# Moving three pieces of work in the order of an attention and mixture-of-experts kernel

## The chip, the cores and the metric

The kernel runs on one core of one Trainium2 chip. The metric is the device time of one execution in microseconds (us). Five engines work side by side, each through its own instructions in order: TensorE (PE, matrix products and transposes), VectorE (DVE), ScalarE (ACT), GpSimd (POOL, which also issues the indirect transfers) and SyncE (SP, which issues plain transfers from its queue). They wait for each other by semaphores.

## The reference

Two stages follow each other. The first is a causal attention with decay, in blocks of 64 positions with a state carried between blocks, for 2 batches, 8 heads, 768 positions and 64 columns per head. Its result, laid out as 1536 tokens of 512 columns, is x of the second: each token goes to the one of 8 experts with the largest logit and comes back weighted by its probability. An expert takes tokens in their order up to its capacity (384).

```python
logits = x @ w_gate
expert_idx = np.argmax(logits, axis=1)
probs = np.exp(logits - logits.max(-1, keepdims=True))
probs /= probs.sum(-1, keepdims=True) + 1e-09
gate_w = probs[np.arange(N), expert_idx]
# tokens kept per expert, in order, up to the capacity: disp[e, pos[i]] = x[i]
h = np.maximum(np.einsum('ecd,edf->ecf', disp, w1), 0.0)
y = np.einsum('ecf,efd->ecd', h, w2)
out[i] = gate_w[i] * y[expert_idx[i], pos[i]]      # for every token that is kept
```

The weights are 8 experts with w1 of 512 by 1024 and w2 of 1024 by 512, in float32.

## The kernel before, in words

**Attention.** The 1536 tokens are worked in 12 ranks of 128 (`NTILE`), six to a batch. Round `s` of the loop in `attention()` works on several ranks at once: scores of rank `s+2` and masks of `s+1` ahead; `attend(s)` and `state(s)` for the rank itself; `turn(s-1)`, which multiplies the finished rank by a permuted identity and the gate's weights and so gives its rows and logits; `choose(s-1)` on VectorE (logits, maximum, index, one-hot `oh`); `rows(s-1)` and `soft(s-1)` on ScalarE (the rows are copied and the sum of exponentials taken); `place(s-2)` on TensorE and `placed(s-2)` on VectorE (the place of each token within its expert), and `scatter(s-2)`: ScalarE turns the places into integers (`slot`) and GpSimd issues an indirect transfer that writes 128 rows to the table `xs` in memory, sorted by expert. The last two ranks are chosen and scattered behind the loop, by the pieces `tail(0)`, `tail(1)` and `tail(2)`, which are put between the matmuls of expert 0's first tile; `count()` then counts the tokens of each expert, and `pad` writes zero rows behind them by indirect transfers.

**Weights.** Each expert has 8 pieces of 128 by 1024. `load_w(i)` loads piece `i` into one of four buffers; `split_hi(i)` rounds it on ScalarE to the precision in which TensorE multiplies at full speed; `split_lo(i)` subtracts on VectorE and keeps the remainder, and frees the buffer. Every product is taken as three: high by high, high by low, low by high. Expert 0's pieces are 0 to 7; 8 to 15 are expert 1's.

**Expert 0.** Its first two tiles of 128 tokens are worked alone, as `Solo` objects `first` and `second`: `turn` transposes the tile's rows, `rest` takes the low part of x, `up(0..3)` are the products with w1, `cross(0..1)` transposes the activations and splits them (`hh` on ScalarE, `hl` on VectorE), `down(0..3)` are the products with w2, `finish` scales by the gate and writes the tokens by an indirect transfer. `first` starts when the tokens of the early ranks have been scattered; `second` needs the rows of all ranks (`load_rows(0, 1)`).

**Experts 1 to 7.** Each takes 232 tokens at once. SyncE reads the expert's rows (`load_rows(e)`, behind the scatters and the pads of that expert), VectorE transposes them (`shuffle(e, g)`, two halves, the first with the token columns `tokens_of`), and `trans(e, g)` splits them into high (ScalarE) and low (VectorE). Expert 1's rows are turned while `second` is worked, those of the later ones during the expert before.

**Order.** The schedule is written out by hand: each engine runs its instructions in the order in which the program issues them. One engine never passes over an instruction that waits. On SyncE, the row reads and the loads of weights are one queue. The tiles of PSUM and of weights are in rings, so that a writer waits for the last reader of the buffer that it takes; `rank` and `st` share one tile, and `turn` writes one tile `tp` that `choose` and `rows` read.

Of the kernel before, what the change touches and what calls it, by code (L numbers as in the profile page):

```python
# [25 lines left out]
NTILE = NT // P  # L26
# [14 lines left out]
LO = {s: s - 5 for s in range(5, 12)}  # L41
# [3 lines left out]
def kernel(  # L45
# [50 lines left out]
    def load_w(i):  # L96
        if i >= E * NWP:
            return
        t = wraw_p.tile([P, WP], F32, tag="wraw", name="wraw")
        nc.sync.dma_start(out=t, in_=wp[i // NWP, i % NWP])  # L100
        raw[i] = t

    def split_hi(i):
        if i >= E * NWP:
            return
        hi = wsp_p.tile([P, WP], F32R, tag="whi", name="whi")
        nc.scalar.activation(out=hi, in_=raw[i], func=AF.Copy)  # L107
        wsp[i] = (hi, None)

    def split_lo(i):  # L110
        if i >= E * NWP:
            return
        t, hi = raw.pop(i), wsp[i][0]
        lo = wsp_p.tile([P, WP], F32R, tag="wlo", name="wlo")
        nc.vector.tensor_tensor(out=lo, in0=t, in1=hi.bitcast(F32), op=ALU.subtract)  # L115
        wsp[i] = (hi, lo)
# [136 lines left out]
    def attention():  # L253
        with ExitStack() as c2:
# [136 lines left out]
            first = Solo(0, spare, spare_ps)  # L391
# [16 lines left out]
            def decay_k(s):  # L408
                if s >= NTILE or s % NC == NC - 1:
                    return  # L410
                kd[s] = p2.tile([P, HP, 2, D], F32, tag="kd", name="kd")
                nc.gpsimd.tensor_tensor(
                    out=kd[s],
                    in0=ld[s, 1][:, 0:DM].rearrange("p (a r d) -> p a r d", a=HP, r=2),
                    in1=dt[:, :, :, P - 1:P].rearrange("p r a o -> p a r o").to_broadcast([P, HP, 2, D]),
                    op=ALU.mult,
                )
# [13 lines left out]
            def mask(s, rs=(0, 1)):  # L431
                if s >= NTILE:
                    return
                if 0 in rs:
                    pt[s] = p3.tile([P, 2, HP, P], F32, tag="pt", name="pt")
                for r in rs:
                    nc.vector.tensor_tensor(out=pt[s][:, r], in0=sc[s][r], in1=dt[:, r], op=ALU.mult)  # L437
# [29 lines left out]
            def carry(s):  # L467

                if s % NC in (0, NC - 1):
                    return  # L470
                tmp[s] = p2.tile([P, HP, D], F32, tag="tmp", name="tmp")
                for a in range(HP):
                    nc.scalar.activation(
                        out=tmp[s][:, a], in_=stt[s][:, a], func=AF.Copy, scale=qp[:, a, P - 1:P]
                    )

            def state(s):
                if s >= NTILE or s % NC == NC - 1:
                    return
                v = ld[s, 1][:, DM:2 * DM].rearrange("p (h d) -> p h d", h=H)  # L480
                for a in range(HP):
                    for r in range(2):
                        nc.tensor.matmul(  # L483
                            st[64 * r:64 * r + 64, a], lhsT=kd[s][:, a, r], rhs=v[:, 2 * a + r],
                            start=True, stop=True,
                        )
                stt[s + 1] = p2.tile([P, HP, D], F32, tag="stt", name="stt")
                if s % NC == 0:
                    nc.vector.tensor_copy(stt[s + 1], st)
                else:  # L490
                    nc.vector.tensor_tensor(out=stt[s + 1], in0=tmp[s], in1=st, op=ALU.add)
# [25 lines left out]
            def choose(s):  # L517
                if s < 0:
                    return
                lg[s] = sm.tile([P, E], F32, tag="l", name="l")  # L520
                nc.vector.tensor_reduce(
                    out=lg[s], in_=tp[s][:, :, P:P + E].rearrange("p k e -> p e k"),
                    axis=mybir.AxisListType.X, op=ALU.add,
                )
                m8[s] = sm.tile([P, 8], F32, tag="m8", name="m8")
                nc.vector.max(out=m8[s], in_=lg[s])
                nc.vector.max_index(out=i8_all[:, s], in_max=m8[s], in_values=lg[s])
                oneh[s] = sm.tile([P, E], F16, tag="oh", name="oh")
                nc.vector.tensor_tensor(  # L529
                    out=oneh[s], in0=nr[s], in1=i8_all[:, s, 0:1].to_broadcast([P, E]), op=ALU.is_equal  # L530
                )
# [17 lines left out]
            def place(s):  # L549
                if s < 0:  # L550
                    return
                nc.tensor.matmul(rank, lhsT=upper, rhs=oneh[s], start=True, stop=False)
                nc.tensor.matmul(rank, lhsT=ones, rhs=cum[s], start=False, stop=(s < EARLY))
                if s >= EARLY:
                    nc.tensor.matmul(rank, lhsT=ones, rhs=more, start=False, stop=True)

            def placed(s):
                if s < 0:
                    return
                pr = sm.tile([P, E], F32, tag="pr", name="pr")  # L560
                nc.vector.scalar_tensor_tensor(
                    out=pr, in0=rank, scalar=1.0, in1=oneh[s], op0=ALU.mult, op1=ALU.mult,
                    accum_out=sraw[:, s:s + 1],
                )
# [11 lines left out]
            def scatter(s):  # L576
                if s < 0:
                    return
                nc.scalar.activation(out=slot[:, s:s + 1], in_=sraw[:, s:s + 1], func=AF.Copy)  # L579
                i = nc.gpsimd.indirect_dma_start(  # L580
                    out=xs, out_offset=bass.IndirectOffsetOnAxis(ap=slot[:, s:s + 1], axis=0),
                    in_=xg_all[:, s], in_offset=None, bounds_check=E * STR - 1, oob_is_err=False,
                )
                apart(i, "xs", s >= EARLY)
# [14 lines left out]
            load(5, 0)  # L599
            tokens()  # L600
            for s in range(NTILE):
                place(s - 2)
                carry(s)
                mask(s + 1, (0,))
                placed(s - 2)
                mask(s + 1, (1,))
                scatter(s - 2)
                decay_k(s + 1)
                if s == NTILE - 1:
                    first.rest()  # L610
                if s in LO:
                    split_lo(LO[s])
                if s > 0:
                    attend(s)
                    state(s)
                if s in HI:
                    split_hi(HI[s])
                turn(s - 1)
                choose(s - 1)
                if s == EARLY + 1:  # L620
                    shift()
                rows(s - 1)
                soft(s - 1)
                if s == NTILE - 2:
                    first.turn()
                score(s + 2)
                if s > 0:
                    load(s + 4, 1)
                for i in LOAD.get(s, ()):
                    load_w(i)  # L630
                decay_q(s + 2)
                add_up(s - 1)
                load(s + 6, 0)
                if s == EARLY - 1:
                    number(slice(NTILE - 2, NTILE))
                if s == EARLY + 1:
                    load_rows(0, 0)
            s = NTILE - 1
# [37 lines left out]
            pad(1, 0)  # L676
            pad(1, 1)
            load_rows(1)
            split_lo(7)
            first.cross(0)  # L680
            split_hi(8)
            first.up(3)
            split_lo(8)
            load_w(11)
            first.down(0)
            first.cross(1)
            split_hi(9)
            split_lo(9)
            load_w(12)
            first.down(1)  # L690
        return first

    def ffn(first):
        with ExitStack() as c2:
# [10 lines left out]
            def shuffle(e, g):  # L705
                if e >= E:
                    return
                if g == 0:
                    tokens_of(e)
                    xf[e] = xf_p.tile([P, KD, RS], F32, tag="xf", name="xf")  # L710
                    xhl[e] = xt_p.tile([P, KD, 2, SLOT], F32R, tag="xhl", name="xhl")
                ks = slice(2 * g, 2 * g + 2)
                nc.vector.transpose(  # L713
                    out=xf[e][:, ks].rearrange("p k (t c) -> p k t c", c=32),
                    in_=rw[e].rearrange("p t (k c) -> p k t c", k=KD)[:, ks],
                )
# [47 lines left out]
            split_w(11)  # L764
            load_w(15)
            second.up(3)
            second.down(0)
            second.cross(1)
            shuffle(1, 0)
            trans(1, 0)  # L770
            shuffle(1, 1)
            trans(1, 1)
# [283 lines left out]
```

## Time and profile before

Three runs took 251.21, 251.28 and 251.78 us; the median is 251.28.

| | |
|---|---|
| profiled execution | 252.51 us |
| its span (first to last instruction) | 250.8 us |
| granted TensorE clock, mean | 0.996 |
| TensorE busy | 237.1 us (95%) |
| VectorE busy | 172.4 us (69%) |
| ScalarE busy | 144.5 us (58%) |
| GpSimd busy | 87.1 us (35%) |
| memory read, written | 50.37 MB, 11.22 MB |

The span is cut by what the core does: ranks of attention to about 59 us, expert 0's first tile with the last choices to about 76, its second tile to about 90, then seven experts of some 21 to 22 us each. Busy times are per engine and overlap. An engine's idle time stands in brackets in a timeline, with the instruction whose end released it. In the chain of waits each piece released the next one.

### The profile page before, as it was taken

The page shows a single profiled execution, that of the slowest core. Times are in us where ns is not written, and L with a number is a line of the kernel's source. Part 1 is how long each engine was busy: PE and PEld are TensorE (multiplying, and loading weights), DVE is VectorE, ACT ScalarE, POOL GpSimd, SP SyncE. Part 2 cuts the span into 40 slices and gives each one's busy share as a digit, 9 for nine tenths or more (in the row PEclk, how much of TensorE's full clock was granted, in tenths as well). Part 3 has the DMA queues.
Part 4 walks back from the last instruction along what each step waited for, and adds up shares of the span by engine and source line. Part 5 has one row for each costly group of instructions (what it writes and reads, how often), then busy time and mean ns, then how long its engine had stood idle before and what let it go on. Part 6 is the DMA issues. An engine that isn't in the chain of part 4 may idle for free.

```text
span 250.8 us, 4968 instructions
## 1 busy us (share of the span) xinstructions
PE 237.1 (95%) x1838; PEld 199.6 (80%) x1838; DVE 172.4 (69%) x323; ACT 144.5 (58%) x267; POOL 87.1 (35%) x105
## 2 busy tenths in 40 slices
PE   7899999999899989999999999999999999999990
PEld 3688888787888979879877977987897788789880
DVE  4555589996474476797679679768866876896400
ACT  2216666788453456568557656855765585586220
POOL 8585769995273502005101600510250030011031
PEclk9999999999999999999999999999999999999998
DMA  5999999958526938867578769859775889462010
GB/s 113 409 370 406 398 381 411 413 176 282 182 71 133 355 122 260 201 220 238 175 236 305 262 141 324 252 178 284 242 249 153 323 236 305 148 231 78 1 54 15
DMA packets 27006, 58.52 MB, mean 233 GB/s; under 512 B 6392, under 2 KB 13562, under 8 KB 26976
## 3 DMA queue, kind: packets, MB, share of 16 engines
q1 hardware_dynamic: 22896, 50.89, 62.5%
q0 software_dynamic: 3376, 7.24, 7.6%
q8 instruction: 16, 0.26, 0.4%
q10 hardware_dynamic: 704, 0.02, 0.2%
q14 instruction: 14, 0.11, 0.1%
HBM read 50.37 MB, written 11.22 MB: 246 GB/s over the span
## 4 chain that ended last, share of the span: by engine, by line
PE 45%; issue 15%; DVE 13%; DMA 11%; ACT 9%; POOL 2%; SPq 1%; POOLq 1%; DVEq 0%; ACTq 0%
PE y L828 13%; PE h L796 10%; DVE wlo L115 6%; DMA wraw<-in_wp 5%; PE h L800 5%; ACT whi L107 5%; PE tp L504 4%; PE sc L429 4%; PE x L449 3%; DMA qk<-in_qkv 3%; DVE hf L806 2%; PE x L457 2%; PE st L483 2%; DVE xhl L724 2%; PE solo_ps L219 1%
## 5 line engine op out<-in xcount | busy, mean ns | idle before, releaser
L115 DVE TENSOR_TENSOR wlo<-wraw,whi 128x1024 fp32r<-128x1024 f32 x64 | 80.9, 1273 | 12.0 <-ACT whi L107 10.1
L796 PE MATMUL h<-xhl,whi 128*128 128x464 f32 x224 | 73.3, 380 | 2.1 <-DVE xhl L724 2.1
L107 ACT ACTIVATE whi<-wraw 128x1024 fp32r<-128x1024 f32 x64 | 66.2, 1047 | 8.7 <-DMA wraw<-in_wp 8.6
L800 PE MATMUL h<-xhl,wlo 128*128 128x232 f32 x224 | 60.2, 269 | 0.0
L183 POOL DMA_INDIRECT out<-y,ti x13 | 15.6, 1196 | 118.3 <-ACT y L837 116.4
L796 PEld LDWEIGHTS h<-xhl,whi 128*128 128x128 f32 x224 | 42.0, 188 | 8.7 <-DVE xhl L724 2.9
L800 PEld LDWEIGHTS h<-xhl,wlo 128*128 128x128 f32 x224 | 42.7, 190 | 0.3
L828 PE MATMUL y<-whi,hh 128*128 128x512 f32 (+1 forms) x104 | 41.1, 396 | 0.0
L828 PE MATMUL y<-whi,hl 128*128 128x512 f32 (+1 forms) x104 | 41.1, 395 | 0.0
L828 PE MATMUL y<-wlo,hh 128*128 128x512 f32 (+1 forms) x104 | 40.9, 393 | 0.0
L809 ACT ACTIVATE hh<-hf 128x464 fp32r<-128x464 f32 x28 | 16.6, 592 | 33.8 <-DVE hf L806 33.8
L810 DVE SCALAR_TENSOR_TENSOR hl<-hf,hh 128x464 fp32r<-128x464 f32 x28 | 18.0, 642 | 18.4 <-ACT hh L809 18.4
L828 PEld LDWEIGHTS y<-whi,hl 128*128 128x128 f32 (+1 forms) x104 | 18.6, 179 | 5.7
L828 PEld LDWEIGHTS y<-wlo,hh 128*128 128x128 f32 (+1 forms) x104 | 18.6, 179 | 5.3
L828 PEld LDWEIGHTS y<-whi,hh 128*128 128x128 f32 (+1 forms) x104 | 18.6, 178 | 5.3
L806 DVE TENSOR_TENSOR hf<-h,hf 128x464 f32<-128x464 f32 x28 | 17.8, 636 | 4.0 <-ACT hf L805 3.3
L580 POOL DMA_INDIRECT xs<-xg,slot x12 | 14.2, 1180 | 11.1 <-ACT slot L579 7.3
L437 DVE TENSOR_TENSOR pt<-sc,dt 128x512 f32<-128x512 f32 x24 | 16.2, 687 | 2.5 <-PE sc L429 2.0
L134 POOL DMA_INDIRECT xs<-zero,padi x14 | 16.1, 1146 | 4.3 <-issue 4.0
L805 ACT ACTIVATE hf<-h 128x464 f32<-128x464 f32 x28 | 15.2, 543 | 2.3 <-PE h L800 2.2
L723 ACT ACTIVATE xhl<-xf 128x464 fp32r<-128x464 f32 x14 | 8.3, 591 | 11.9 <-DVE xf L713 11.9
L513 ACT ACTIVATE xg<-tp 128x512 f32<-128x512 f32 x12 | 7.2, 598 | 13.5 <-DVE oh L529 11.7
(133 smaller groups left out, 349.6 us busy)
## 6 DMA issues: line engine op xcount, KB each, us to landing
wraw<-in_wp SPq DMA_DIRECT2D x64, 512.0 KB
qk<-in_qkv SPq DMA_DIRECT2D x12, 512.0 KB
kv<-in_qkv SPq DMA_DIRECT2D x12, 512.0 KB
rw<-xs SPq DMA_DIRECT2D x28, 128.0 KB
xs<-xg SPq DMA_DIRECT2D x1, 514.0 KB
rw<-xs SPq DMA_DIRECT2D x2, 257.0 KB
xs<-zero,padi POOLq DMA_INDIRECT x14, 3.5
out<-y,ti POOLq DMA_INDIRECT x13, 4.0
```

What stands on the lines that cost most here:

```text
L107: nc.scalar.activation(out=hi, in_=raw[i], func=AF.Copy)
L115: nc.vector.tensor_tensor(out=lo, in0=t, in1=hi.bitcast(F32), op=ALU.subtract)
L134: i = nc.gpsimd.indirect_dma_start(out=xs, out_offset=bass.IndirectOffsetOnAxis(ap=padi[:, e, t:t + 1], axis=0), in_=zero, in_offset=None, ...
L183: i = nc.gpsimd.indirect_dma_start(out=out, out_offset=bass.IndirectOffsetOnAxis(ap=ti[e][0:m, t:t + 1], axis=0), in_=y[0:m], in_offset=No ...
L437: nc.vector.tensor_tensor(out=pt[s][:, r], in0=sc[s][r], in1=dt[:, r], op=ALU.mult)
L796: nc.tensor.matmul(ps[:, f, 0:2 * SLOT], lhsT=wh[:, k, fs], rhs=x2[:, k], start=(k == 0), stop=False, skip_group_check=True,)
L800: nc.tensor.matmul(ps[:, f, 0:SLOT], lhsT=wl[:, k, fs], rhs=x2[:, k, 0], start=False, stop=(k == KD - 1), skip_group_check=True,)
L805: nc.scalar.activation(out=hf, in_=ps[:, :, SLOT:2 * SLOT], func=AF.Copy)
L806: nc.vector.tensor_tensor(out=hf, in0=ps[:, :, 0:SLOT], in1=hf, op=ALU.add)
L809: nc.scalar.activation(out=hh, in_=hf, func=AF.Relu)
L810: nc.vector.scalar_tensor_tensor(out=hl, in0=hf, scalar=0.0, in1=hh.bitcast(F32), op0=ALU.max, op1=ALU.subtract)
L828: nc.tensor.matmul(yp[t][0:m], lhsT=a[:, f, tsl], rhs=b[:, f], start=(p == 0 and f == 0 and n == 0), stop=(p == 3 and f == 1 and n == 2),)
```

## The change

Three things are moved; no instruction is added or taken away.

1. In the last round of the loop (`s` = 11), `place(9)`, `placed(9)` and `scatter(9)` come behind `attend(11)` instead of ahead of it (`carry`, `mask` and `decay_k` do nothing in that round), and `split_lo(6)` comes behind `choose(10)` instead of ahead of the attention. `first.rest()` is then the round's first work on VectorE.
2. Behind the loop, `split_lo(7)` is issued behind `first.up(3)` instead of ahead of `first.cross(0)`, and `split_lo(8)` behind `first.cross(1)` instead of ahead of `first.down(0)`. `load_w(12)` comes two steps earlier in the program, behind `split_lo(8)`; `split_lo(9)` comes behind `first.down(1)`.
3. In expert 0's second tile, `shuffle(1, 0)`, the first half of expert 1's transposition, comes ahead of `second.down(0)` and `second.cross(1)`.

```diff
@@ -599,24 +599,31 @@
             load(5, 0)
             tokens()
             for s in range(NTILE):
-                place(s - 2)
-                carry(s)
-                mask(s + 1, (0,))
-                placed(s - 2)
-                mask(s + 1, (1,))
-                scatter(s - 2)
-                decay_k(s + 1)
-                if s == NTILE - 1:
+                if s < NTILE - 1:
+                    place(s - 2)
+                    carry(s)
+                    mask(s + 1, (0,))
+                    placed(s - 2)
+                    mask(s + 1, (1,))
+                    scatter(s - 2)
+                    decay_k(s + 1)
+                    if s in LO:
+                        split_lo(LO[s])
+                else:
                     first.rest()
-                if s in LO:
-                    split_lo(LO[s])
                 if s > 0:
                     attend(s)
                     state(s)
+                if s == NTILE - 1:
+                    place(s - 2)
+                    placed(s - 2)
+                    scatter(s - 2)
                 if s in HI:
                     split_hi(HI[s])
                 turn(s - 1)
                 choose(s - 1)
+                if s == NTILE - 1:
+                    split_lo(LO[s])
                 if s == EARLY + 1:
                     shift()
                 rows(s - 1)
@@ -676,18 +683,18 @@
             pad(1, 0)
             pad(1, 1)
             load_rows(1)
-            split_lo(7)
             first.cross(0)
             split_hi(8)
             first.up(3)
-            split_lo(8)
+            split_lo(7)
             load_w(11)
             first.down(0)
             first.cross(1)
+            split_lo(8)
+            load_w(12)
             split_hi(9)
+            first.down(1)
             split_lo(9)
-            load_w(12)
-            first.down(1)
         return first
 
     def ffn(first):
@@ -764,9 +771,9 @@
             split_w(11)
             load_w(15)
             second.up(3)
+            shuffle(1, 0)
             second.down(0)
             second.cross(1)
-            shuffle(1, 0)
             trans(1, 0)
             shuffle(1, 1)
             trans(1, 1)
```

## Rows read from the trace of the kernel before

**Rows 1.** TensorE's waits from 56 us to the end: us in total, times, longest.
```profile
PE h L796 <- DVE xhl L724: 2.1, 3, 0.9
```
**Rows 2.** Timeline of TensorE: start, us, instructions, idle time before.
```profile
59.35 0.17 PE L552 MATMUL st<-oh,upper 128*128 128x8 f16 x1 [0.59 <-DVE m L526]
61.12 0.18 PE L502 MATMUL tp<-num,warm 128*128 128x8 f16 x1
64.05 0.17 PE L552 MATMUL st<-oh,upper 128*128 128x8 f16 x1 [0.78 <-DVE oh L529]
64.74 0.17 PE L502 MATMUL tp<-num,warm 128*128 128x8 f16 x1
76.17 0.63 PE L200 MATMUL solo_ps<-ident,rw 128*128 128x128 f32 x4 [0.61 <-DMA rw<-xs]
91.93 0.47 PE L796 MATMUL h<-xhl,whi 128*128 128x464 f32 x1 [0.94 <-DVE xhl L724]
```
**Rows 3.** Timeline of VectorE, last round of the loop.
```profile
61.09 0.69 DVE L205 TENSOR_TENSOR solo_xl<-solo_ps,solo_xh 128x512 fp32r<-128x512 f32 x1 [1.29 <-ACT slot L579]
62.02 1.21 DVE L115 TENSOR_TENSOR wlo<-wraw,whi 128x1024 fp32r<-128x1024 f32 x1
63.14 0.18 DVE L521 TENSOR_REDUCE l<-tp 128x8 f32<-128x32 f32 x1
63.84 0.17 DVE L529 TENSOR_TENSOR oh<-tp,i 128x8 f16<-128x8 f32 x1
64.31 0.17 DVE L561 SCALAR_TENSOR_TENSOR pr<-st,oh 128x8 f32<-128x8 f32 x1 [0.31 <-PE st L555]
```
**Rows 4.** Timeline of ScalarE, last round of the loop.
```profile
60.41 0.57 ACT L202 ACTIVATE solo_xh<-solo_ps 128x512 fp32r<-128x512 f32 x1
64.09 0.60 ACT L513 ACTIVATE xg<-tp 128x512 f32<-128x512 f32 x1 [1.29 <-DVE oh L529]
```
**Rows 5.** Timeline of GpSimd: indirect transfers issued.
```profile
68.98 1.97 POOL L580 DMA_INDIRECT xs<-xg,slot  x1 [1.69 <-ACT slot L579]
71.26 1.97 POOL L134 DMA_INDIRECT xs<-zero,padi  x1 [0.30 <-DVE solo_hl L232]
73.53 0.97 POOL L134 DMA_INDIRECT xs<-zero,padi  x1 [0.30 <-issue]
...
140.32 0.99 POOL L134 DMA_INDIRECT xs<-zero,padi  x1 [0.30 <-issue]
```
**Rows 6.** Timeline of VectorE beside those transfers.
```profile
68.86 1.22 DVE L115 TENSOR_TENSOR wlo<-wraw,whi 128x1024 fp32r<-128x1024 f32 x1
70.21 0.69 DVE L232 TENSOR_TENSOR solo_hl<-solo_ps,solo_hh 128x512 fp32r<-128x512 f32 x1
71.16 1.23 DVE L115 TENSOR_TENSOR wlo<-wraw,whi 128x1024 fp32r<-128x1024 f32 x1 [0.26 <-ACT whi L107]
...
140.74 1.23 DVE L115 TENSOR_TENSOR wlo<-wraw,whi 128x1024 fp32r<-128x1024 f32 x1 [0.30 <-ACT whi L107]
```
**Rows 7.** Timeline of SyncE's queue: the row reads.
```profile
73.27 0.33 SPq L167 DMA_DIRECT2D rw<-xs  x1
76.82 1.81 SPq L152 DMA_DIRECT2D rw<-xs  x4
```
**Rows 8.** Chain of waits: start, us, what.
```profile
79.22 4.51 DMA wraw<-in_wp
```
**Rows 9.** Timeline of ScalarE, second expert's weights.
```profile
83.87 1.06 ACT L107 ACTIVATE whi<-wraw 128x1024 fp32r<-128x1024 f32 x1 [0.27 <-DMA wraw<-in_wp]
```
**Rows 10.** Timeline of VectorE from the second tile to expert 1.
```profile
77.52 0.69 DVE L205 TENSOR_TENSOR solo_x<-solo_ps,solo_x 128x512 fp32r<-128x512 f32 x1 [1.88 <-ACT solo_x L202]
84.97 1.23 DVE L115 TENSOR_TENSOR wlo<-wraw,whi 128x1024 fp32r<-128x1024 f32 x1 [0.64 <-ACT whi L107]
86.89 0.69 DVE L232 TENSOR_TENSOR solo_hl<-solo_ps,solo_hh 128x512 fp32r<-128x512 f32 x1 [0.70 <-ACT solo_hh L231]
87.94 0.71 DVE L713 STREAM_TRANSPOSE xf<-rw 128x512 f32<-128x512 f32 x1
```

## The prediction

> **What bounds the kernel now.** I began with the page: TensorE is busy 95% of the span at full clock, so what is left to win there is its gaps. TensorE's waits come next. Behind the eleventh round of the loop the largest entry, 2.1 us in three waits, is the experts' matmul held by VectorE's `xhl` [rows 1]; the timeline puts 0.94 us of it at 91.93, the start of expert 1. Three other gaps stand in the same timeline: 0.59 at 59.35 and 0.78 at 64.05 (ranks waiting for a choice) and 0.61 at 76.17 (the second tile of expert 0 waiting for its row read) [rows 2]. Then the chain of waits, followed back from 91.93: VectorE's transposition and low part for expert 1, weight piece 11 and its load at 79.22 [rows 8], SyncE's row read of expert 1 at 76.82 [rows 7], two `pad` transfers on GpSimd [rows 5], and before them the last two choices. So the stretch from 59 to 92 us is bound by one chain across all engines, which touches TensorE at four gaps, 2.92 us in sum. All three edits lie on it.
>
> **Step 1, the loop's last round.** Before, `place(9)` waits on TensorE till 59.35, then attention and `turn(10)` follow, the latter at 61.12 [rows 2]. After, `attend(11)` starts when the transposes are over, at 59.35 - 0.59 = 58.76, and nothing that it reads is late; with the same 1.77 us for attention and rank, `turn(10)` starts near 60.5. That alone gives nothing: `choose(10)` is on VectorE, in order, behind `first.rest()` and `split_lo(6)`. There the first low part of x starts at 61.09, since it waits for ScalarE's copy (60.41 + 0.57) [rows 3, 4]; this is unchanged. At 62.02 `split_lo(6)` begins, and the choice starts at 63.14 [rows 3]. After, the place of `split_lo` is taken by `placed(9)`, which came earlier before: one 0.17 us instruction [rows 3] and its readout, together 0.2 as I take them. `choose(10)` then starts at 62.2 and, at the same 0.87 us (63.14 to 63.84 + 0.17), ends at 63.07 instead of 64.01: 0.94 us sooner. `split_lo(6)` runs from 63.1 to 64.3, beside matmuls, and delays `placed(10)` to 64.3, which is where it stands now (64.31) [rows 3].
>
> Not all of the 0.94 reaches TensorE. `turn(11)` (64.74) writes the tile that `rows(10)` reads, so it waits for that copy to end, 64.09 + 0.60 [rows 2, 4]. ScalarE is in order: `slot(9)` now waits for `placed(9)` till 62.3, `split_hi(7)` stands behind it (the same copy takes 1.06 in rows 9), so `rows(10)` starts near 63.4, not at 63.1. `turn(11)` comes at 64.0: gain **0.72 us**. Everything behind it (third part of `up`, last choice, `count`) follows TensorE and shifts alike. Bounds: 0.94 if ScalarE doesn't hold it, zero if `slot(9)` is some 0.7 later than I think. The moved `scatter(9)` issues near 62.8 instead of its old place ahead of the choices; its successors on GpSimd, `add_up(10)` and `scatter(10)`, are wanted by `place(11)` past 66 only. SyncE's load of weight 10, which needs `split_lo(6)`, slips about 1.1 us; its row reads are not due until 71, so they lose nothing.
>
> **Step 2, the low parts 7 and 8.** An indirect transfer on GpSimd takes 0.97 to 0.99 when nothing is in the way. The last scatter at 68.98 and the first pad at 71.26 take 1.97 [rows 5]. Each began just behind the start of a `split_lo` on VectorE (68.86, 1.22; 71.16, 1.23), and each ends 0.84 to 0.87 us behind that `split_lo`'s end [rows 5, 6]. The pad at 73.53 had no `split_lo` running and took 0.97. One that has begun isn't caught: at 140.32 a pad took 0.99 though a `split_lo` began at 140.74 [rows 5, 6]. So the rule of the rows: a transfer that begins inside a `split_lo` waits for its end, then needs 0.84. By it, after the edit:
> - Last scatter: 68.98 - 0.72 = 68.26, no `split_lo` beside it, ends 69.24. First pad 0.30 later, 69.54 to 70.5. `split_lo(7)` is still issued by VectorE as soon as the crossing's low part `hl` is done (70.21 + 0.69 - 0.72 = 70.18), since nothing it reads is late: it does not stay behind the third `up`. It catches the second pad, which begins at 70.8, holds it till 71.4, and the pad ends at 72.2 instead of 74.50.
> - Row read of expert 0's second tile: 73.27 less 0.72 less 0.99 = 71.56 [rows 7]. Its data were what TensorE got at 76.17; 1.71 earlier is 74.46. TensorE itself arrives at 76.17 - 0.61 - 0.72 = 74.84. The gap of **0.61 us** goes whole, with 0.38 to spare; what is late next there is TensorE's own work.
> - Row read of expert 1: 76.82 less 2.3 = 74.5, and weight 11 behind it loads from 76.9 instead of 79.22; at the same 4.51 us [rows 8] it lands at 81.4.
> - `split_lo(8)` follows the second crossing. VectorE stood idle for 1.88 us ahead of the second tile's low part of x at 77.52 [rows 10]; less the 0.61 that TensorE no longer waits, 1.27 are left for the 1.23 of `split_lo(8)`. It just fits; were it late by x, the tile's first `up` would lose at most x, and I take nothing.
>
> The Trainium skill speaks against step 2. Its page "SBUF — State Buffer", section "Who interferes with whom", says that a two-input `tensor_tensor` did not stall DMAs in its probe, because it takes only the read side of the port pair shared with GpSimd and the writing of descriptors needs the write side (marked as inferred); the same section says that such an instruction does contend with a GpSimd instruction that reads SBUF. By the first sentence moving `split_lo` frees no transfer and the sum would lose the 0.61; by the second, and by the two 1.97 us transfers of this trace, it does. I go by the rows.
>
> **Step 3, the shuffle ahead of the crossing.** Now VectorE does `split_lo(11)` (84.97, 1.23), the crossing's low part (86.89, 0.69), the token columns and the first transposition (87.94, 0.71), and from 87.94 a chain of two transpositions, copies and low parts releases TensorE at 91.93 [rows 2, 10]. After, weight 11 is there in time: its high part, which waited 0.27 for the load [rows 9], starts at 83.60 - 1.33 = 82.3, the low part ends near 84.6 (it began 1.10 behind the high part), the token columns take at most 0.44 (86.89 to 87.94 less the 0.61 after which the next can follow a low part) [rows 10], and the transposition is done at about 85.7. The crossing's low part is due at 86.89 - 1.33 = 85.56: at most 0.15 late, and I take nothing for it. The transposed rows are there 2.9 us earlier (88.65 to 85.7), so the chain, with nothing else on its way, would end near 89.0. TensorE wants it at 91.93 - 0.94 - 1.33 = 89.66: the **0.94 us** go as well. By bounds: none if the chain came 1.6 us later than I reckon, 0.94 at most.
>
> **Sum.** 0.72 + 0.61 + 0.94 = 2.27 us. The profiled execution took 252.51 (span 250.8 and 1.7 around it), so 250.24 in its terms; the runs have a median of 251.28, and I take the same amount off: **249.0 us**. Behind 92 us the instructions are the same, TensorE runs on without a gap but for the other 1.2 us of those three waits [rows 1], and loads are asked for by freed buffers, so the shift should carry to the end.
>
> **Rivals.**
> - *The rows' rule is a coincidence; transfers aren't freed (the skill's first sentence).* The row read moves by 0.72 only, the 0.61 gap stays, weight 11 moves by 0.72, and the shuffle pushes the crossing's low part back by up to 0.43. Gain 0.72 + 0.94 less 0.43 at worst: 1.2 to 1.7, time 249.6 to 250.1. For it: nothing in the trace; against it: both 1.97 transfers.
> - *The front gives nothing.* If ScalarE's order (`slot(9)`, `split_hi(7)`, `rows(10)`) costs all of step 1, the other two remain: 1.55, 249.7.
> - *More than that.* The other two waits of [rows 1], 1.2 us later on, depend on when loads land; if the shift happens to remove them, 248.0.
> - *The gain is given back at an expert's boundary*: an earlier chain asks for loads that land when they landed before. 250.6 to 251.6. Against it: the row reads and loads of this stretch are queued behind transfers that move too.
> - *Slower.* Five more expert boundaries each read new rows and weights behind pads. If the new phase of pads against `split_lo` made each of them wait as at 91.93, five times 0.94 less the 1.2 now there, 3.5 us, would come on: 252.5. It decides from 0.46 us more per boundary (2.27 over five). Against it: these stretches keep their own order on every engine.
>
> **How the numbers follow.** Chances: forecast 0.62 (own range 248.6 to 249.5), more 0.08, rule a coincidence 0.08, front gives nothing 0.09, given back 0.08, slower 0.05. A difference counts from 0.3%, 0.75 us, which is about what can be told from no change: the first four are faster (0.87), then same 0.08, slower 0.05. The range from 248.2 to 250.2 leaves out most of the last two cases and about half of "more".
>
> **What would show it.** In the changed profile: `attend(11)` ahead of the rank with no 0.59 gap; `choose(10)` starting near 62.2 and `turn(11)` near 64.0; last scatter and first pad under 1.05 us, second pad near 1.4; no gap ahead of the second tile's transposes; weight 11's load near 76.9; no gap in expert 1's first piece; then the same work some 2.3 us earlier. It would be wrong if the scatters still take 1.97 with no `split_lo` beside them, if `turn(11)` stays at 64.7, or if a wait for `xhl` longer than 0.9 appears at a later boundary.

## The result, and the profile after

The changed kernel takes 248.72 us (median of 4 runs, 247.08 to 249.20) against 251.25 for the kernel before; the ratio is 0.9884, with an interval from 0.9839 to 0.9928. On another chip it was 248.13 against 251.15, 0.9896 (0.9849 to 0.9943). 249.0 had been forecast. The profiled execution took 248.73 (span 246.9) against 252.51 (250.8): 3.8 less, of which only 2.85 belong to the three steps, as the table below shows.

TensorE's waits from 56 us to the end (us in total, times, longest): of the six behind [rows 1, 2], one is left.

```profile
PE st L552 <- DVE oh L529: 0.5, 1, 0.5
```

The timeline of TensorE, for [rows 2]: attention follows the transposes with no gap, the rank comes behind it, the second tile's transposes and expert 1's third pair of matmuls (89.25) wait for nothing.

```profile
58.77 1.09 PE L449 MATMUL x<-pt,kv 128*64 128x128 f32 x16
60.39 0.18 PE L552 MATMUL st<-oh,upper 128*128 128x8 f16 x1
63.09 0.17 PE L552 MATMUL st<-oh,upper 128*128 128x8 f16 x1 [0.47 <-DVE oh L529]
63.98 0.17 PE L502 MATMUL tp<-num,warm 128*128 128x8 f16 x1
74.64 0.60 PE L200 MATMUL solo_ps<-ident,rw 128*128 128x128 f32 x4
89.25 0.38 PE L803 MATMUL h<-xhl,whi 128*128 128x464 f32 x1
```

VectorE's timeline in the loop's last round and beside the last choices, for [rows 3, 6]. The choice starts at 62.17 instead of 63.14, right behind `placed(9)`; `split_lo(6)` runs behind it, `split_lo(7)` right behind the crossing's low part.

```profile
62.10 0.15 DVE L561 SCALAR_TENSOR_TENSOR pr<-st,oh 128x8 f32<-128x8 f32 x1
62.17 0.19 DVE L521 TENSOR_REDUCE l<-tp 128x8 f32<-128x32 f32 x1
62.95 1.22 DVE L115 TENSOR_TENSOR wlo<-wraw,whi 128x1024 fp32r<-128x1024 f32 x1
...
69.44 0.69 DVE L232 TENSOR_TENSOR solo_hl<-solo_ps,solo_hh 128x512 fp32r<-128x512 f32 x1 [1.26 <-ACT solo_hh L231]
70.05 1.22 DVE L115 TENSOR_TENSOR wlo<-wraw,whi 128x1024 fp32r<-128x1024 f32 x1
```

ScalarE's timeline, for [rows 4]: `slot(9)` waits for `placed(9)`, `split_hi(7)` stands behind it, and `rows(10)` comes at 63.35, not at 64.09.

```profile
62.29 0.21 ACT L579 ACTIVATE slot<-sraw 128x1 int32<-128x1 f32 x1 [0.73 <-DVE pr L561]
62.40 1.04 ACT L107 ACTIVATE whi<-wraw 128x1024 fp32r<-128x1024 f32 x1
63.35 0.58 ACT L513 ACTIVATE xg<-tp 128x512 f32<-128x512 f32 x1
```

GpSimd's timeline, for [rows 5]: the last scatter and first pad take 0.99 and 0.97 instead of 1.97; the second pad, which begins inside `split_lo(7)`, ends at 72.11, 0.84 behind that instruction's end (71.27).

```profile
68.21 0.99 POOL L580 DMA_INDIRECT xs<-xg,slot  x1 [1.69 <-ACT slot L579]
69.51 0.97 POOL L134 DMA_INDIRECT xs<-zero,padi  x1 [0.30 <-issue]
70.79 1.32 POOL L134 DMA_INDIRECT xs<-zero,padi  x1 [0.30 <-issue]
```

SyncE's queue, for [rows 7, 8]: the second tile's row read is issued at 71.01 (73.27 before), expert 1's at 74.47 (76.82), weight 11's load at 76.89 (79.22).

```profile
71.01 0.33 SPq L167 DMA_DIRECT2D rw<-xs  x1
74.47 1.82 SPq L152 DMA_DIRECT2D rw<-xs  x4
76.33 0.45 SPq L157 DMA_DIRECT2D wt<-xs  x1
76.89 14.66 SPq L100 DMA_DIRECT2D wraw<-in_wp  x7
```

VectorE ahead of expert 1, for [rows 10]: the transposition ends at 85.29, just as the crossing's low part falls due (85.31), and the chain ends at 88.52, before TensorE asks.

```profile
83.00 1.23 DVE L115 TENSOR_TENSOR wlo<-wraw,whi 128x1024 fp32r<-128x1024 f32 x1 [0.25 <-issue]
...
84.58 0.71 DVE L720 STREAM_TRANSPOSE xf<-rw 128x512 f32<-128x512 f32 x1
85.31 0.69 DVE L232 TENSOR_TENSOR solo_hl<-solo_ps,solo_hh 128x512 fp32r<-128x512 f32 x1
...
87.88 0.64 DVE L731 TENSOR_TENSOR xhl<-xf,xhl 128x464 fp32r<-128x464 f32 x1 [0.66 <-ACT xhl L730]
```

For the comparison of executions I read from each TensorE timeline when the work of a stage starts. The attention's start-up shifts from one execution to the next (by up to 1.6 us in those here), so each column is set against the start of `state(10)`'s matmuls, which is put at the 56.49 us of before. A boundary, below, is the change from one expert to the next. The last two columns belong to the later boundaries: the time from expert 2's start to expert 7's, and TensorE's idle times (its brackets) at the starts.

| execution | `turn(11)` | second tile | expert 1 | expert 2 | expert 2's start to 7's | waits at the starts of experts 2 to 7 |
|---|---|---|---|---|---|---|
| before | 64.74 | 76.17 | 90.19 | 112.85 | 109.32 | 0.39, 0.74 |
| before, again (e4) | 64.74 | 75.58 | 90.32 | 112.98 | 109.32 | 0.22, 0.86 |
| changed | 63.90 | 74.56 | 88.53 | 110.00 | 108.11 | none |
| changed, again (e9) | 63.89 | 74.54 | 88.51 | 109.98 | 108.68 | 0.19 |
| step 1 alone (e1) | 63.89 | 74.93 | 88.92 | 111.58 | 110.28 | 0.33, 0.78, 0.87 |
| step 2 alone (e2) | 64.74 | 75.41 | 89.44 | 112.09 | 110.60 | 1.12, 0.90, 0.27 |
| step 3 alone (e3) | 64.73 | 75.88 | 90.76 | 112.23 | 108.60 | 0.39 |
| changed, early pads (e11) | 63.90 | 74.56 | 88.71 | 110.18 | 107.83 | none |

By the start of expert 2 the change is worth 112.85 - 110.00 = 2.85 us (2.98 against before, again). From there on the order is the same; what differs are waits that come and go.

### The profile page after: what moved, and what is told of

Same layout as the page of the kernel before. It is cut to its first block, busy times and chain, and to the rows that moved or that the text cites. A ratio compares the mean times of both kernels' runs of the same rounds, so it can differ in the third digit from the quotient of the medians.

```text
span 246.9 us, 4966 instructions
## 1 busy us (share of the span) xinstructions
PE 235.2 (95%) x1838; PEld 199.3 (81%) x1838; DVE 172.0 (70%) x323; ACT 144.7 (59%) x267; POOL 86.6 (35%) x105
## 4 chain that ended last, share of the span: by engine, by line
issue 55%; PE 20%; POOL 8%; DMA 4%; POOLq 4%; ACT 3%; DVE 3%; SPq 0%; DVEq 0%; ACTq 0%
POOL xs L134 5%; PE tp L504 4%; PE sc L429 4%; PE x L449 3%; POOLq L896 3%; DMA qk<-in_qkv 3%; POOL out L183 2%; PE solo_y L243 2%; PE solo_ps L219 2%; PE x L457 2%; PE st L483 2%; DMA lam_q<-in_lam 1%; DVE wlo L115 1%; ACT whi L107 1%; ACT xg L513 1%
## 5 line engine op out<-in xcount | busy, mean ns | idle before, releaser
L580 POOL DMA_INDIRECT xs<-xg,slot x12 | 13.2, 1102 | 11.8 <-ACT slot L579 8.0
L429 PE MATMUL sc<-qk 64*128 64x128 f32 x192 | 14.3, 285 | 1.7 <-DMA qk<-in_qkv 1.7
L429 PEld LDWEIGHTS sc<-qk 64*128 64x128 f32 x192 | 11.9, 187 | 4.1 <-DMA qk<-in_qkv 1.7
```

What stands on the lines that cost most here:

```text
L429: nc.tensor.matmul(sc[s][r][:, a], lhsT=kT[rs, a], rhs=qT[rs, a], start=True, stop=True)
```

## The experiments

**Each step alone.** The edits are the hunks of the diff shown above: e1 has the loop's, e2 that of the low parts 7 and 8, e3 the shuffle's.

> Step 1 of the change alone (last round of the loop, split_lo(6) behind choose(10)). Theory (three parts of one chain, each with its own gap): turn(11) comes 0.7 to 0.85 us earlier, the 0.61 us gap ahead of the second tile and the 0.94 us gap at expert 1 stay, so 0.7 to 0.9 us faster. Rival (what fills the gaps is the pads' chain; the front is worth nothing alone): under 0.3 us, with the gap ahead of the second tile grown to more than 1.2 us.

Measured: 251.36 against 252.35, ratio 0.9963 (0.9932 to 0.9993). `turn(11)` comes 0.85 earlier; expert 1's gap stays at 0.94, the second tile's at 0.21 of 0.61. Expert 2 starts 1.27 to 1.40 earlier than in the two executions of before, more than expected, since the second tile's gap shrank instead of staying and, against e4, since weight 11 was there in time at the second crossing. TensorE's timeline of e1:

```profile
74.97 0.63 PE L200 MATMUL solo_ps<-ident,rw 128*128 128x128 f32 x4 [0.21 <-DMA rw<-xs]
90.69 0.47 PE L803 MATMUL h<-xhl,whi 128*128 128x464 f32 x1 [0.94 <-DVE xhl L731]
```

> Step 2 alone (split_lo(7) and split_lo(8) moved). Theory: last scatter and first pad take 0.97 to 1.0 us instead of 1.97, the gap ahead of the second tile goes, 0.6 to 0.8 us faster; the gap at expert 1 stays at 0.9, since the crossing's low part and not the load sets the shuffle. Rival (a two-input tensor_tensor doesn't hold an indirect transfer): scatter and pad stay at 1.97 and the time stays within 0.3 us.

Measured: 251.48 against 252.35, ratio 0.9958 (0.9922 to 0.9994). The second tile waits for nothing, expert 1 waits 0.92, expert 2 starts 0.76 earlier (0.89 against e4). This execution's later boundaries lost 2.3 us to waits, so its single time would have shown no gain. GpSimd's timeline of e2:

```profile
69.02 0.99 POOL L580 DMA_INDIRECT xs<-xg,slot  x1 [1.69 <-ACT slot L579]
70.31 0.97 POOL L134 DMA_INDIRECT xs<-zero,padi  x1 [0.30 <-issue]
71.59 1.33 POOL L134 DMA_INDIRECT xs<-zero,padi  x1 [0.30 <-issue]
```

> Step 3 alone (shuffle(1, 0) ahead of the second crossing). Theory: the gap at expert 1 goes (0.94 by its bracket, about 1.1 from start to start), less up to 0.4 because weight 11 is still late and the shuffle pushes the crossing's low part back: 0.7 to 1.1 us faster. Rival (the shuffle needs the earlier load of step 2): the low part holds TensorE in down(2) by 0.5 or more and the gain is under 0.4 us.

Measured: 251.30 against 252.35, ratio 0.9949 (0.9915 to 0.9983). Expert 1's matmuls take 21.47 from its start to expert 2's instead of 22.66: 1.19 less. Its start is 0.44 to 0.57 later, though, and mostly not because of the shuffle. Weight 11 landed late, `split_hi(11)` stood on ScalarE ahead of the copy that the crossing needs, and TensorE waited there, as it also did in the kernel before, again (0.53, e4). The shuffle's own cost is small and stands in no bracket: it pushed the crossing's low part back to 87.74, 0.4 behind its high part's end, and in `down(2)` the first product with that low part started 0.31 and the one behind it 0.34 after its forerunner, instead of 0.23 each, so 0.19 was lost. ScalarE and TensorE of e3:

```profile
84.43 1.06 ACT L107 ACTIVATE whi<-wraw 128x1024 fp32r<-128x1024 f32 x1 [1.05 <-DMA wraw<-in_wp]
85.39 0.58 ACT L224 ACTIVATE solo_raw<-solo_ps 128x512 f32<-128x512 f32 x1
86.03 0.66 PE L229 MATMUL solo_ps<-ident,solo_raw 128*128 128x128 f32 x4 [0.46 <-ACT solo_raw L224]
...
88.14 0.40 PE L243 MATMUL solo_ps<-wlo,solo_hh 128*128 128x512 f32 x1
88.45 0.50 PE L243 MATMUL solo_ps<-whi,solo_hl 128*128 128x512 f32 x1
88.79 0.40 PE L243 MATMUL solo_ps<-whi,solo_hh 128*128 128x512 f32 x1
```

By the start of expert 2 the three alone give 1.27, 0.76 and 0.62, 2.65 in sum, against 2.85 together. So the steps add, nearly; no one of them needs another to count.

> The kernel before, unchanged. Theory: the two waits for the rows of expert 3 and expert 6 (0.39 and 0.68 us in the profiled execution of before) come and go between executions and are no property of the order; this profile has other ones or none, and the timed runs spread by about 1 us. Rival (they belong to the old order and the change removed them): they stand at the same two places with 0.3 us or more each.

Measured: 252.58 against 252.35 for the other runs of the same kernel, ratio 1.001 (0.9973 to 1.0047), its runs from 250.82 to 254.58. The theory fell in part: waits stand at the same two boundaries, experts 3 and 6 (0.22 and 0.86; the profile of before has 0.39 and 0.74, not 0.68). But e1 and e2, whose order there is the same, have theirs at experts 4, 5 and 6, and e3 has one at 6 alone.

**What holds the transfers.** The kernel before, with

```diff
-            split_lo(7)
+            low_from_psum(7, first.hn[0])
...
-            split_lo(8)
+            low_from_psum(8, first.hn[1])
+    def low_from_psum(i, ps):
+        t, hi = raw.pop(i), wsp[i][0]
+        lo = wsp_p.tile([P, WP], F32R, tag="wlo", name="wlo")
+        for c in range(2):
+            cs = slice(DM * c, DM * c + DM)
+            nc.vector.tensor_tensor(out=lo[:, cs], in0=ps, in1=t[:, cs], op=ALU.subtract)
+        wsp[i] = (hi, lo)
```

> The kernel before with its old order, but split_lo(7) and split_lo(8) read one input from PSUM (two instructions of 128x512 each, a product tile instead of the high part), so the low parts of pieces 7 and 8 hold other numbers than the reference wants; the work on VectorE stays about as long. Theory (an indirect transfer is held by a VectorE instruction with both inputs in SBUF, here split_lo): last scatter and pads take 0.97 to 1.05 us each though VectorE is as busy beside them, and the gap ahead of the second tile goes; 0.3 to 0.9 us faster. Rival (any long VectorE instruction holds it): last scatter and first pad still end some 0.85 us behind VectorE's instruction, 1.6 to 2.0 each.

This kernel leaves out the true low parts of pieces 7 and 8 and is read for its timing only. Measured: the last scatter began at 69.74, inside a stretch of VectorE from 69.63 to 70.91, and took 0.99. Both pads took 0.97, but neither began inside one of the altered instructions, so the scatter alone is the test. VectorE and GpSimd of e5:

```profile
69.63 1.28 DVE L123 TENSOR_TENSOR wlo<-solo_ps,wraw 128x512 fp32r<-128x512 f32 x2
```

```profile
69.74 0.99 POOL L588 DMA_INDIRECT xs<-xg,slot  x1 [1.68 <-ACT slot L587]
71.04 0.97 POOL L142 DMA_INDIRECT xs<-zero,padi  x1 [0.30 <-DVE wlo L123]
```

The edit also cut each instruction to half its length (two of 0.64), so by itself it leaves open whether the input or the length counts. Two pads of e10 (described below) settle that. One began 0.10 into a VectorE instruction of 0.63 with one input in PSUM (`h`) and took 0.97; the other began 0.09 into one of 0.64 with both inputs in SBUF (`hf`, `hh`) and took 1.40, ending 0.85 behind it. VectorE and GpSimd of e10:

```profile
98.20 0.63 DVE L809 TENSOR_TENSOR hf<-h,hf 128x464 f32<-128x464 f32 x1
99.49 0.64 DVE L813 SCALAR_TENSOR_TENSOR hl<-hf,hh 128x464 fp32r<-128x464 f32 x1 [0.66 <-ACT hh L812]
```

```profile
98.30 0.97 POOL L134 DMA_INDIRECT xs<-zero,padi  x1 [0.30 <-issue]
99.58 1.40 POOL L134 DMA_INDIRECT xs<-zero,padi  x1 [0.30 <-issue]
```

So it is not any long VectorE instruction that holds a transfer, but one with both inputs in SBUF, a short one too. The gap at the second tile did not go but shrank to 0.28, and the time, 252.22 against 252.40, ratio 0.9979 (0.9949 to 1.001), is not told from no change; `split_lo` in its new form waits for two product tiles and this execution lost 2.9 us at later boundaries.

> The changed kernel with split_lo(7) alone put back ahead of the first crossing. Theory: last scatter back at 1.97, pads free; row read of the second tile 1.0 us later than in the changed kernel, so its data come some 0.6 us behind TensorE's arrival at the second tile, or less where they land early: a gap of 0.1 to 0.6 there, and 0.1 to 0.7 us slower than the changed kernel. Rival (the pads, not the scatter, carry the gain): no gap at the second tile.

The edit moves the one line `split_lo(7)` back ahead of `first.cross(0)`. Measured: the last scatter is at 1.97 again, both pads take 0.97, and the second tile waits. GpSimd and TensorE of e6:

```profile
68.40 1.97 POOL L580 DMA_INDIRECT xs<-xg,slot  x1 [1.68 <-ACT slot L579]
70.68 0.97 POOL L134 DMA_INDIRECT xs<-zero,padi  x1 [0.31 <-DVE solo_hl L232]
```

```profile
75.63 0.63 PE L200 MATMUL solo_ps<-ident,rw 128*128 128x128 f32 x4 [0.65 <-DMA rw<-xs]
```

The scatter alone makes that gap. The trace's loss is larger than expected, and not all of it is the scatter's: counted as in the table, the second tile starts 0.79 later than in the changed kernel and expert 1 2.03 later, because expert 1's row read was issued 3.27 behind the second pad's end instead of 2.36 and weight 11 came late with it (TensorE waited 0.78 at the second crossing). This profiled execution is the slowest of the thirteen, at 255.02. The median is 250.31 against 252.40, ratio 0.9906 (0.9871 to 0.9941), which overlaps the changed kernel's interval; the loss is shown by the trace only.

**What is left.** The last gap on TensorE ahead of `place(10)`, and the waits at later boundaries:

```diff
                 choose(s - 1)
                 if s == NTILE - 1:
+                    tokens_of(0, 0)        # no longer in first.rest()
                     split_lo(LO[s])
...
                 soft(s - 1)
+                if s == NTILE - 1:
+                    split_hi(HI[s])        # no longer ahead of turn(s - 1)
```

> The changed kernel with the token columns of the first tile behind choose(10) and split_hi(7) behind soft(10). Theory (the one gap left on TensorE, 0.47 us ahead of place(10), is VectorE's order, and turn(11) waits for ScalarE's order): place(10) 0.3 us earlier, turn(11) 0.3 to 0.5 us earlier than in the changed kernel, and as much off the time. Rival (TensorE is full behind it and something else sets the end): turn(11) earlier, but the start of the second tile or of expert 1 where it was.

Measured: the gap falls from 0.47 to 0.15, `turn(11)`, the second tile and expert 1 all start 0.52 earlier (63.38, 74.04, 88.01). The time, 249.50 against 252.40, ratio 0.9894 (0.9859 to 0.9929), doesn't tell it from the changed kernel.

```diff
             load_rows(2)
+            for e in range(4, E):
+                pad(e, 0)
+                pad(e, 1)
...
-                    pad(e + 3, 0)
-                    pad(e + 3, 1)
```

> The changed kernel with the pads of experts 4 to 7 all issued at the start of expert 1 instead of behind each expert's end. Theory (the waits of 0.2 to 1.1 us at the boundaries of experts 2 to 7, which come and go, arise because SyncE's queue stands some 7 us behind each pad with the weight loads behind it): no wait for xhl behind expert 1, the row reads no longer wait for pads, and the timed runs lie at or below the best ones of the changed kernel, 1 us or so below its median. Rival (the waits come from slow loads themselves): boundary waits as before, time as the changed kernel's.

Measured: no wait at any boundary, 248.03 against 252.40, ratio 0.9817 (0.9777 to 0.9856). SyncE's waits tell why (us in total, times, longest): in the changed kernel its queue stands 28.3 us for pads at four boundaries, with the weight loads behind them, and ScalarE then waits 4.3 for loads. Of the changed kernel, from 93 us on:

```profile
SPq L152 <- DMA xs<-zero,padi: 28.3, 4, 7.3
...
ACT whi L107 <- DMA wraw<-in_wp: 4.3, 4, 1.2
```

With early pads both entries are gone, here and in e10 to e12.

> The changed kernel, unchanged, on the chip of the other three runs. Theory (about 2.85 us by the start of expert 2 in every execution, boundary waits on top that come and go in both kernels): 2.5 to 3 us faster than before; expert 1's matmuls take 21.5 us, expert 2 starts 2.5 to 2.9 us earlier than in the kernel before; waits for xhl at one or more later boundaries may stand in this profile. Rival (the change removes the boundary waits): none again.

Measured: 248.13 against 251.15, ratio 0.9896; expert 2 starts 2.87 earlier than in before, and one boundary wait of 0.19 is there. So the change doesn't remove all of these waits; that its first profile had none was luck, and part of the 3.8 us between the two profiled executions (109.32 - 108.11 = 1.2) is this. Whether the change makes them rarer stays open: a wait at the start of expert 6 (0.27 to 1.30) stands in all seven executions with late pads that lack a step or part of one (before, e1 to e6), and in none of the three with the whole change and late pads (changed, e7, e9).

> The kernel before with the pads of experts 4 to 7 issued at the start of expert 1. Theory (boundary waits come from SyncE's queue standing behind pads, in either order of the front): no wait at the boundaries of experts 2 to 7, the gaps at 59, 64, 76 and 92 us as before; 0.7 to 2 us faster than before. Rival (the pads matter only with the new front): boundary waits remain, time as before.

Measured: 250.08 against 251.15, ratio 0.9966 (0.9938 to 0.9994). No boundary wait, and the starts of experts 2 to 7 stand 21.52 to 21.60 apart, with the old front as it was, but for the second tile's gap, which is 0.20 here.

> The changed kernel with the early pads once more, beside the changed kernel itself. Theory: no boundary waits, experts 2 to 7 start 21.5 to 21.6 us apart, 0.7 to 1.5 us faster than the changed kernel on this chip. Rival: within 0.3 us of the changed kernel.

Measured: 248.42, no faster than the changed kernel's 248.13 beside it. The mechanism is as expected (no boundary wait, 107.83 from expert 2 to 7), the gain isn't. From expert 2 to 7 the changed kernel lost only 0.9 on this chip (108.68 - 107.83), of which 0.19 is a bracket, and here expert 1 starts 0.2 later: weight 11 was split some 0.4 later, the crossing's low part, now behind the shuffle, came late with it, and `down(2)` lost 0.15, again without a bracket.

> Both additions to the changed kernel: early pads, and the token columns behind choice(10) with split_hi(7) behind soft(10). Theory: their gains add, turn(11) 0.5 us earlier and no boundary waits, 0.4 to 0.6 us faster than the early pads alone, the fastest of all. Rival: the 0.5 us is lost behind turn(11).

Measured: 246.68 (246.50 to 247.56), ratio 0.9839 (0.9805 to 0.9872): the lowest median of all, 1.45 under the changed kernel beside it, though the intervals overlap. It is 1.74 under e11, more than expected, and the traces don't explain that by the theory. Its profile shows the rival instead: `turn(11)` is at 63.39 and the second tile at 74.05, but expert 1 starts at 88.77, since weight 11, issued at 76.34, landed only at 82.3, and TensorE waited at the second crossing as in e3. Counted as in the table, expert 7 starts at 218.07, in e11 at 218.01; of the 1.09 between these two executions, about 1.0 lies behind the last write's issue. So the gain of the earlier choice is lost again in this execution, and the cause of the lower median stays open. ScalarE and TensorE of e12:

```profile
82.32 1.06 ACT L107 ACTIVATE whi<-wraw 128x1024 fp32r<-128x1024 f32 x1 [0.92 <-DMA wraw<-in_wp]
83.91 0.66 PE L230 MATMUL solo_ps<-ident,solo_raw 128*128 128x128 f32 x4 [0.34 <-ACT solo_raw L225]
```

## Why the prediction was right

- *Step 1, 0.72 forecast:* the gain is 0.84 by the table. The instructions came where they were put: choice at 62.17 (62.2 forecast), `rows(10)` at 63.35 (63.4), `turn(11)` at 63.98 (64.0); the rest of the difference is that the whole execution began 0.08 later.
- *Step 2, 0.61:* the second tile starts 1.61 earlier, 0.77 beyond step 1. Last scatter 68.21 (68.26), pads 69.51 (69.54) and 70.79 (70.8), weight 11's load 76.89 (76.9). The rule that a transfer begun inside a `split_lo` waits for its end held in all fourteen profiles, with one exception: in e1 a pad that began only 0.04 into `split_lo(11)` took 0.97. The first ones held began 0.09 into theirs. e5 and e10 narrow the rule to VectorE instructions with two SBUF inputs, so the rival that it is a coincidence fell. The Trainium skill, "SBUF — State Buffer", "Who interferes with whom", states that a VectorE instruction with two SBUF inputs contends with a GpSimd instruction that reads SBUF, and these traces agree (1.40 against 0.97 in e10); that it is the reading of the row numbers, which lie in SBUF, that waits is not shown. What the same section reports of its probe, in which `tensor_tensor` did not stall a transfer, doesn't hold for these.
- One number of step 2 failed without harm: the row read was issued at 71.01, not at 71.56. The forecast kept the time from the scatter's end to the read that waits for its landing at what the profile of before had, 2.32; it is 1.81 in the changed kernel and 1.80 in e4. So the 0.61 was partly the luck of one profile and is no fixed gap: in e4 the second tile started only 0.18 behind the matmul's due time, with no bracket, and 0.53 stood at the second crossing instead. At the start of expert 1 both executions of before agree within 0.13, so the sum of steps 1 and 2 is firmer than its parts.
- *Step 3, 0.94:* expert 1's matmuls take 1.19 less (22.66 to 21.47). The forecast took nothing for the crossing's low part, which now stands behind the shuffle. That held in the changed kernel (85.31, right behind it), but cost 0.15 to 0.19 where weight 11 came late (e3, e11, e12).
- *The size.* The steps gave 0.12, 0.16 and 0.25 more than the sum had. Step 1's 0.12 lies in its chain of single instructions; no bracket entered its 0.72. Steps 2 and 3 took brackets as prices. The bracket ahead of an instruction counts from the modelled end of the one before, but without the wait the next matmul would have started before that end. At 76.17 the one before had started at 75.18 and the next was due 0.23 later: 0.76. At 91.93 the one before had started at 90.72 and the next was due 0.11 later, at 90.83: 1.10; and the first matmul after a wait held its successor 0.32 instead of 0.21. Together 1.2, which is what step 3 gained. TensorE of the kernel before:

```profile
90.72 0.26 PE L800 MATMUL h<-xhl,wlo 128*128 128x232 f32 x1
...
92.25 0.27 PE L800 MATMUL h<-xhl,wlo 128*128 128x232 f32 x1
```

- *The time.* The gain is 2.85 at expert 2 against 2.27 forecast, and 2.5 and 3.0 in the medians of two chips. The rivals "front gives nothing" and "given back" fell by e1 and the table. "More" was half right: the later waits do hang on when loads land, but a wait occurs with the change too (0.19 in e9, 0.60 in e7). By its own sum it is 247.8, not 248.0. "Slower" has no support: with the whole change no wait longer than 0.60 stands at a boundary, and kernels that lack a step have up to 1.31.

What stays open is why these waits fall at other boundaries from one execution to the next, and the spread of 2 to 4 us between timed runs, of which the traces show three parts (start-up, boundary waits, the end).

## What to carry to other kernels

Price a gap on the busiest engine from start to start of its instructions, not by the idle time before them, and in more than one execution: the second tile's was 0.77 in one profile of the kernel before and 0.18 in the next. Before an indirect transfer that others wait for, keep VectorE off instructions with two SBUF inputs: 1.2 us of them cost the transfer up to 1.0. A queue that issues loads should not also wait for a late small transfer: in the changed kernel it stood some 7 us at each of four boundaries.

## What the runs showed of the hardware that was not expected

From the start of the last write's issue to the end of the span, the fourteen profiled executions fall into two groups whatever the kernel: 4.7 to 4.8 us (e3, e5, e8, e10, e12) and 5.7 to 6.3 (before, changed, e1, e2, e4, e6, e7, e9, e11). A 512 KB load behind the row reads took 4.5 us to land in one execution (before) and about 5.9 in another (e12). From the end of an indirect transfer on GpSimd to the issue of the read that waits for it, the fourteen executions took 1.80 to 2.32 us behind the last scatter and 1.98 to 3.55 behind expert 1's second pad.
